# Attention and MLP in one kernel: w_out brought to one scale, both rows of a block bent at once, small factors on GpSimd, and a new order of the last products

## The chip, the cores and the metric

The kernel runs on one core of a Trainium2 chip. The core has TensorE (PE in the profile; its weight loads are PEld), VectorE (DVE), ScalarE (ACT), GpSimd (POOL) and SyncE (SP), which issues most DMAs. The metric is device microseconds of one execution, the median of several runs; lower is better.

## The reference

There are 8 batches of 12 heads, each with 448 rows of 64. Cut to what matters:

```python
scores = np.matmul(q, k.transpose(0, 1, 3, 2)) / np.sqrt(64) - np.log(448)
attn = np.matmul(1.0 / (1.0 + np.exp(-scores)), v)          # sigmoid, no softmax
x = attn.transpose(0, 2, 1, 3).reshape(3584, 768)
h = x @ w_in                                                # 768 x 2048
g = np.where(h >= 1, h, np.where(h <= -1, 0, (h + 1) ** 2 / 4))
out = g @ w_out                                             # 2048 x 768
```

## The kernel before, in words

**Numbers.** Products are made of f16 matmuls: each f32 factor is scaled by a power of two (found from its largest value) and split into a high and a low f16 part, and hi·hi, hi·lo and lo·hi are summed in PSUM. So each matrix product is three matmuls.

**Attention.** The 12 heads of a batch are 6 pairs, 48 in all. A pair has four pieces: three of 128 keys and one of 64. Scores of the first pairs are plain f32 matmuls (L407); later ones are L411, L416 and L425, of which L425 uses half the rows of the array (64). ScalarE makes the sigmoid (L454, L457), splits it (L465) and VectorE takes the low part (L466), which frees the PSUM bank of scores; there are two. The product with v is L498, which uses half the columns of the array (64). `prep_a` loads a pair (tile `raw`) and finds its largest values, on ScalarE (L344) for pairs below MAX_ACT and on VectorE (L346) for the others; `prep_b` makes the scales (L131 to L139, L359, L360) and splits q, k and v, on VectorE (L373, L374) or on GpSimd (L378 to L380). Corners of keys are copied on GpSimd (L437).

**The first product.** Of batches 0 and 1 it is plain (`up`, L722: chunk f of the 16 chunks of 128 columns of w_in against all six row chunks of x). From batch 2 (SB) on it is made of block products (`up_blocks`, L688): w_in chunks i and i + 8 and the two halves of x and of the 448 columns are combined so that 7 products of quarter size replace 8; each of the 8 values of i takes 63 matmuls of 224 columns, and the quarters are added up by VectorE (L697) and ScalarE. The combined weights are made once, during batch 1 (`mix`, L622 to L658), written to DRAM and loaded for each i (`load_set`, L664).

**Bending.** `bend` turns h into g, once for each chunk: ScalarE's Relu with scale ihr and bias hr (L735), VectorE's min and multiply (L736) and multiply and max (L737), ScalarE's f16 copy (L738), VectorE's low part (L739).

**The second product.** `down` (L758): six rows m of 128 outputs, for each eight units u; a unit is a pair of chunks of g (u and u + 8 from batch 2 on) with six matmuls. VectorE scales the result (L768), SP stores it.

**Scales.** The chunks of w_in and w_out form two groups (NA = 8), each with a scale of its own. The factors that this needs are 128x1 operations on VectorE, made by `small` (L553 to L557): for batch 1 in `common_scales`, from batch 2 on in `block_scales`, which calls it. `finish_x` and `finish_blocks` make the scale of x of the next batch first (L131 to L139, tiles x_e, x_s, x_i).

**Order.** The first stage loads and converts both weights (`convert`, L218 to L247; clamps at L226, on GpSimd or VectorE by CLAMP; `split`, L282 to L287), with the attention of batches 0 and 1 beside it. The main loop then goes over the batches: the units of the first product, then those of the second, and between them the pieces of the attention of the next batches, by a share. A scheduler orders each engine's instructions by priorities; blocks carry a raised one (Q_PRIO). Constants say how much of each kind goes to which engine and when.

Of the kernel before, what the change touches and what calls it, by code (L numbers as in the profile page):

```python
# [23 lines left out]
P = 128  # L24
# [12 lines left out]
NA = 8  # L37
# [13 lines left out]
MAX_ACT = 47  # L51
L0 = 9
# [4 lines left out]
CLAMP = 7  # L57
# [18 lines left out]
def sigmoid_attention_mlp(ctx: ExitStack, tc: tile.TileContext, first_qvk, qkv, w_in, w_out, out_t):  # L76
# [48 lines left out]
    def scales(m, n, tag, pool=None, square=False, less=0):  # L125

        pool = pool or sml_p
        few = {"bufs": 1} if tag == "x" else {}
        mask, top = (EXP_MASK - EXP_ONE, TOP - 1) if square else (EXP_MASK, TOP - less)
        e = sml_p.tile([P, 3], F32, tag="e", name=tag + "_e")[:, :n]  # L130
        nc.vector.tensor_scalar(out=e, in0=m, scalar1=TINY, scalar2=None, op0=ALU.max)  # L131
# [7 lines left out]
        nc.vector.tensor_scalar(  # L139
            out=inv.bitcast(I32), in0=ei, scalar1=float(top * EXP_ONE), scalar2=None, op0=ALU.subtract  # L140
        )
        return s, inv
# [9 lines left out]

    def all_sum(m, n, pm=None):

        mb = sml_p.tile([P, 3], BF16, tag="mb", name="mb", bufs=1)[:, :n]
        nc.vector.tensor_copy(out=mb, in_=m)
        if pm is None:
            pm = ps_mo.tile([P, 512], F32, tag="mo", name="pm")
        nc.tensor.matmul(pm[:, :n], ones, mb, start=True, stop=True)
        return pm[:, :n]  # L160
# [18 lines left out]
    class Weight:  # L179
# [74 lines left out]
        def find_scale(self):  # L254
# [298 lines left out]
    def small(tag, in0, s1, op0, s2=None, op1=None, ints=False):  # L553
        t = sml_p.tile([P, 1], F32, tag=tag, name=tag, bufs=2 if tag.startswith("od") else 1)
        o, i = (t.bitcast(I32), in0.bitcast(I32)) if ints else (t, in0)
        nc.vector.tensor_scalar(out=o, in0=i, scalar1=s1, scalar2=s2, op0=op0, **({"op1": op1} if op1 else {}))
        return t  # L557
# [108 lines left out]
    def block_scales(b, inv_x):  # L666

        common_scales(b, small("invq", inv_x, 0.25, ALU.mult), small("ihc", inv_x, mixed["inv"], ALU.mult))


    PRODUCTS = (0, 0, 0), (3, 4, 1), (5, 5, 2), (6, 3, 3), (1, 1, 0), (2, 6, 2), (4, 2, 3)

    def up_blocks(b, i, j):
# [20 lines left out]
        hf, hg = (rows[:, (i % 2 * 2 + k) * S : (i % 2 * 2 + k + 1) * S] for k in range(2))  # L694
# [3 lines left out]
        with tc.high_priority(offset=Q_PRIO):  # L698
# [3 lines left out]
            elif j == 3:  # L702
                add(u3, 2, u2)
                add(hg[:, HN:], 3, u3)
# [11 lines left out]
    def up(b, f, u):  # L716
# [23 lines left out]

    part = drm_p.tile([NCC, P, S], F32, name="part")

    def down(b, m, u, k):

        lo, hi = (0, NFC) if k is None else (GROUPS[k].start, GROUPS[k].stop)
        if u == 0:
            hold["po"] = ps_mo.tile([P, 512], F32, tag="mo", name="po")
            hold["o"] = out_p.tile([P, S], F32, tag="o", name="o")
            if m == 0:
                hold["od"] = down_sc[b, k]()  # L750
            if k == 1:
                nc.sync.dma_start(out=hold["o"], in_=part[m])
        po, o = hold["po"], hold["o"]
# [104 lines left out]
    for u, unit in enumerate(units):  # L858
# [108 lines left out]
```

## Time and profile before

| | us |
| --- | --- |
| median of 3 runs | 1190.68 |
| lowest and highest | 1190.14, 1194.91 |
| profiled execution | 1187.38 |
| its span | 1185.7 |
| PE busy | 1144.9 (97%) |
| DVE busy | 854.9 (72%) |
| ACT busy | 697.6 (59%) |
| POOL busy | 332.8 (28%) |

The span runs from the first to the last instruction of the profiled execution; its time has 1.7 us around that. The busy shares are averages over a first stage, in which weights are converted, and seven batches that repeat. The waits are those that the profile could find for each instruction, with what ended them. In the groups of instructions the number behind the bar is the busy time in all and the mean of one in ns. A timeline row gives start, length, engine, line, operation and, behind an x, how many in a row.

### The profile page before, as it was taken

The numbers are of one execution on the slowest core, as the hardware profiler recorded it, in microseconds if no ns is written. First come the engines' busy times: TensorE is split into PE (matmuls) and PEld (weight loads), VectorE is DVE, ScalarE is ACT, GpSimd is POOL, SyncE is SP. The second block draws the span as 40 slices with busy tenths as digits, with TensorE's granted clock in tenths as the row PEclk, the third lists the DMA queues.
The fourth block names the chain that finished last, engine by engine and source line by source line (L and its number), as shares of the span: only waits on it lengthen the run. The fifth ranks groups of instructions, "written<-read, shape, count | busy, mean of one in ns | idle before, by whom it ended". The sixth has DMA issues, their size and how long they took to land.

```text
span 1185.7 us, 20268 instructions
## 1 busy us (share of the span) xinstructions
PE 1144.9 (97%) x7662; PEld 669.3 (56%) x7662; DVE 854.9 (72%) x1828; ACT 697.6 (59%) x1158; POOL 332.8 (28%) x393
## 2 busy tenths in 40 slices
PE   5889899999999999999999999999999999999998
PEld 1224333444445776457754677557764577558954
DVE  6999999999956588457973689456884678736830
ACT  5886576665654577547864578455864476613510
POOL 3004410011323244234345235332532353310000
PEclk9899999999999999999999999999999999999999
DMA  9842354437542266224643065423552246302400
GB/s 367 322 153 76 118 161 152 134 119 257 182 148 72 95 217 210 76 72 142 238 163 102 30 236 208 135 64 128 204 211 64 65 147 220 126 24 87 163 16 32
DMA packets 58113, 170.01 MB, mean 143 GB/s; under 512 B 8608, under 2 KB 39840, under 8 KB 51872
## 3 DMA queue, kind: packets, MB, share of 16 engines
q1 hardware_dynamic: 56288, 159.29, 39.1%
q10 hardware_dynamic: 1728, 9.44, 2.2%
q8 instruction: 60, 0.98, 0.3%
q14 instruction: 37, 0.30, 0.1%
HBM read 126.94 MB, written 23.40 MB: 127 GB/s over the span
## 4 chain that ended last, share of the span: by engine, by line
PE 71%; DVE 17%; DMA 4%; ACT 3%; issue 2%; POOL 2%; SPq 0%; POOLq 0%; ACTq 0%; DVEq 0%
PE po L758 33%; PE ph L688 22%; PE pav L498 8%; PE psc L416 3%; PE psc L425 2%; PE ph L722 2%; DVE g L736 2%; PE psc L411 1%; DVE g L737 1%; DVE ghl L739 1%; DMA raw<-qkv 1%; DVE ahl L466 1%; DVE w_in_sb L244 1%; DVE mixa L632 1%; DVE w_out_sb L247 1%
## 5 line engine op out<-in xcount | busy, mean ns | idle before, releaser
L758 PE MATMUL po<-ghl,w_out_sb 128*128 128x448 f16 x2304 | 446.3, 353 | 1.5 <-DVE qkv_e L131 0.6
L758 PEld LDWEIGHTS <-w_out_sb 128*128 128x128 f16 x2304 | 221.7, 98 | 219.4 <-issue 15.9
L688 PE MATMUL ph<-w_in_sb 128*128 128x224 f16 x3024 | 307.7, 259 | 1.3 <-DVE g L737 0.9
L688 PEld LDWEIGHTS <-w_in_sb 128*128 128x128 f16 x3024 | 282.6, 98 | 30.1 <-issue 27.2
L466 DVE SCALAR_TENSOR_TENSOR ahl<-psc,ahl 128x896 f16<-128x896 f32 (+1 forms) x170 | 153.0, 900 | 105.7 <-ACT ahl L465 103.6
L378 POOL TENSOR_SCALAR raw<-raw,qkv_s 128x448 f32<-128x448 f32 (+1 forms) x93 | 71.0, 777 | 449.9 <-DVE qkv_i L139 346.3
L457 ACT ACTIVATE psc<-psc,nls,sqk 128x896 f32<-128x896 f32 (+1 forms) x136 | 129.5, 971 | 103.5 <-PE psc L425 86.6
L465 ACT ACTIVATE ahl<-psc 128x896 f16<-128x896 f32 (+1 forms) x170 | 126.9, 762 | 29.8 <-DVE ahl L466 28.6
L722 PE MATMUL ph<-xhl,w_in_sb 128*128 128x448 f16 x576 | 114.5, 356 | 4.7 <-DVE g L737 3.4
L344 ACT ACTIVATE dump<-raw 128x448 f16<-128x448 f32 (+1 forms) x105 | 61.9, 589 | 85.8 <-DMA raw<-qkv 84.5
L697 DVE TENSOR_TENSOR xhl<-ph,xhl 128x224 f32<-128x224 f32 x240 | 87.7, 383 | 25.3 <-PE ph L688 19.4
L738 ACT ACTIVATE ghl<-g 128x448 f16<-128x448 f32 x128 | 72.5, 573 | 44.2 <-DVE g L737 43.8
L498 PE MATMUL pav<-ahl,v 128*64 128x448 f16 x748 | 95.6, 360 | 0.0
L735 ACT ACTIVATE g<-xhl,hr,ihr 128x448 f32<-128x448 f32 x96 | 68.7, 752 | 41.9 <-DVE xhl L697 41.0
L722 PEld LDWEIGHTS <-w_in_sb 128*128 128x128 f16 x576 | 55.7, 99 | 63.6 <-issue 14.4
L736 DVE SCALAR_TENSOR_TENSOR g<-g,rk 128x448 f32<-128x448 f32 x112 | 81.4, 741 | 10.2 <-ACT g L735 10.0
L739 DVE TENSOR_TENSOR ghl<-g,ghl 128x448 f16<-128x448 f32 x128 | 85.0, 672 | 5.3 <-ACT ghl L738 4.8
L768 DVE TENSOR_SCALAR o<-po,od 128x448 f32<-128x448 f32 x48 | 32.5, 679 | 61.1 <-PE po L758 60.8
L380 POOL TENSOR_TENSOR hl<-raw,hl 128x448 f16<-128x448 f32 x62 | 71.1, 1167 | 0.0
L416 PE MATMUL psc<-qk 128*128 128x448 f16 x252 | 66.3, 354 | 2.0 <-ACT a L454 1.0
L737 DVE SCALAR_TENSOR_TENSOR g<-xhl,ihs,g 128x448 f32<-128x448 f32 x96 | 66.3, 708 | 0.3
L498 PEld LDWEIGHTS <-v 128*64 128x64 f16 x748 | 36.3, 109 | 37.9 <-issue 23.0
(167 smaller groups left out, 1198.5 us busy)
## 6 DMA issues: line engine op xcount, KB each, us to landing
w_in_sb<-blocks SPq DMA_DIRECT2D x48, 1344.0 KB, 6.1
raw<-qkv SPq DMA_DIRECT2D x34, 704.0 KB, 4.7
qk<-hl SPq DMA_DIRECT2D x320, 56.0 KB, 2.0
w_out_sb<-w_in SPq DMA_DIRECT2D x16, 768.0 KB, 8.5
out_t<-o SPq DMA_DIRECT2D x48, 224.0 KB, 1.9
blocks<-mixs SPq DMA_DIRECT2D x8, 768.0 KB, 3.5
w_out_sb<-w_out ACTq DMA_DIRECT2D x6, 768.0 KB, 4.1
raww<-w_out ACTq DMA_DIRECT2D x6, 768.0 KB, 5.7
```

The costliest lines, as they stand in the source:

```text
L416: nc.tensor.matmul(out, kq[:, j, 1, w], kq[:, j, 0, :], start=True, stop=False)
L457: nc.scalar.activation(a, a, AF.Sigmoid, bias=nls, scale=sqk)
L465: nc.scalar.activation(hi, x, AF.Copy, scale=ATT)
L466: nc.vector.scalar_tensor_tensor(out=lo, in0=x, scalar=ATT, in1=hi, op0=ALU.mult, op1=ALU.subtract)
L498: nc.tensor.matmul(pav[j * D : (j + 1) * D, :S], *terms[j][t], start=c == 0 and t == 0, stop=mid and t == len(terms[j]) - 1,)
L688: nc.tensor.matmul(out, w[:, wt, wh, c * P : (c + 1) * P], xc[:, xt, c, xh, :], start=j in (0, 2) and c + wh + xh == 0, stop=c == HC - 1 a ...
L697: add = lambda out, q, other: nc.vector.tensor_tensor(out=out, in0=quarter(q), in1=other, op=ALU.add)
L722: nc.tensor.matmul(ph[:, :S], w_in_sb[:, f, wh, c * P : (c + 1) * P], xhl[:, c, xh, :], start=c == 0 and wh + xh == 0, stop=c == NCC - 1 a ...
L736: nc.vector.scalar_tensor_tensor(out=g, in0=g, scalar=rt, in1=g, op0=ALU.min, op1=ALU.mult)
L737: nc.vector.scalar_tensor_tensor(out=g, in0=h, scalar=ihs, in1=g, op0=ALU.mult, op1=ALU.max)
L739: (nc.gpsimd if f % GPOOL else nc.vector).tensor_tensor(out=ghl[:, f, 1, :], in0=g, in1=hi, op=ALU.subtract)
L758: nc.tensor.matmul(po[:, :S], w_out_sb[:, f, wh, m * P : (m + 1) * P], ghl[:, f, gh, :], start=f == lo and wh + gh == 0, stop=f == hi - 1 ...
```

## The change

- **GpSimd's factors.** From batch 1 on `small` issues on GpSimd, but for the bitwise and.
- **One scale for w_out.** When w_out's scales are known, `even_out` makes a common one; during the blocks' first units of batch 2, `even_chunks` multiplies w_out's f16 parts in place to it, two chunks in one VectorE operation of 128x3072, eight in all. `block_scales` then needs one set of factors for both groups.
- **bend_two** bends rows i and i + 8 of a block in one go: each of its operations is 128x896, and the last additions of the block become one of 128x448. The quarters 2 and 3 change places.
- **Order of the second product.** From batch 2 on rows m = 0 and m = 1 take their units u = 0 to 5 first, then u = 6 and 7 of m = 0, then of m = 1.
- **Shares.** Three clamps of w_in (L226) and 48 corner copies (L437) go from GpSimd to VectorE, the largest values of eleven more pairs (MAX_ACT) from ScalarE to VectorE; L0, MIX1, WO_B and Q_PRIO shift loads, mixing, conversion and priorities.

```diff
-WO_B = 66
+WO_B = 63
-MAX_ACT = 47
-L0 = 9
+MAX_ACT = 36
+L0 = 17
-CLAMP = 7
+CLAMP = 1
-CORN = 10
+CORN = 38
+TE = 4
+CUT = 6
+TWO = 0
+EV0 = 12
-MIX1 = 85
-Q_PRIO = 72
+MIX1 = 95
+Q_PRIO = 12
...
-        nc.vector.tensor_scalar(out=o, in0=i, scalar1=s1, scalar2=s2, op0=op0, **({"op1": op1} if op1 else {}))
+        (nc.gpsimd if state.get("late") and TE & 4 and op0 != ALU.bitwise_and else nc.vector).tensor_scalar(out=o, in0=i, scalar1=s1, scalar2=s2, op0=op0, **({"op1": op1} if op1 else {}))
...
-        common_scales(b, small("invq", inv_x, 0.25, ALU.mult), small("ihc", inv_x, mixed["inv"], ALU.mult))
+        invq, ihc = small("invq", inv_x, 0.25, ALU.mult), small("ihc", inv_x, mixed["inv"], ALU.mult)
+        rt = small("qm", *(largest(invq, k)[1] for k in range(2)), ALU.min)
+        up_sc[b, 0] = up_sc[b, 1] = sc = up_scales(ihc, rt, 0)
+        od = small("od", inverse("ig", sc[4]), even["inv"], ALU.mult)
+        down_sc[b, None] = lambda: od
...
+    def even_chunks(f, n):
+        w = w_out_sb[:, f : f + n].rearrange("p f h n -> p (f h n)")
+        k = int(f >= NA)
+        nc.vector.tensor_scalar(out=w, in0=w, scalar1=evens[:, 2 + k : 3 + k], scalar2=None, op0=ALU.mult)
...
-    PRODUCTS = (0, 0, 0), (3, 4, 1), (5, 5, 2), (6, 3, 3), (1, 1, 0), (2, 6, 2), (4, 2, 3)
+    PRODUCTS = (0, 0, 0), (3, 4, 1), (5, 5, 3), (6, 3, 2), (1, 1, 0), (2, 6, 3), (4, 2, 2)
...
-                add(hg[:, :HN], 2, u2)
-                add(hf[:, HN:], 3, u2)
+                both = h[:, HN : HN + S].rearrange("p (r n) -> p r n", r=2)
+                halves = hold[i, 2].rearrange("p (r n) -> p r n", r=2)[:, :, :HN]
+                other = u2.rearrange("p (r n) -> p r n", r=1).to_broadcast([P, 2, HN])
+                nc.vector.tensor_tensor(out=both, in0=halves, in1=other, op=ALU.add)
         if j == 6:
-            bend(b, i + NFC // 2, hg)
-            bend(b, i, hf)
+            bend_two(b, i, h)
+
+    def bend_two(b, i, h):
+
+        ihr, hr, rt, ihs, _ = up_sc[b, 0]
+        g = raw_p.tile([P, 2 * DM], I32, tag="raww", name="g2").bitcast(F32)[:, : 2 * S]
+        hi, lo = (ghl[:, i :: NFC // 2, k, :] for k in range(2))
+        g2 = g.rearrange("p (r n) -> p r n", r=2)
+        nc.scalar.activation(g, h, AF.Relu, bias=hr, scale=ihr)
+        nc.vector.scalar_tensor_tensor(out=g, in0=g, scalar=rt, in1=g, op0=ALU.min, op1=ALU.mult)
+        nc.vector.scalar_tensor_tensor(out=g, in0=h, scalar=ihs, in1=g, op0=ALU.mult, op1=ALU.max)
+        nc.scalar.activation(hi, g2, AF.Copy)
+        nc.vector.tensor_tensor(out=lo, in0=g2, in1=hi, op=ALU.subtract)
...
-        return [lambda m=m, u=u: down(b, m, u, k) for m in range(NCC) for u in range(n // 2)]
+        order = [(m, u) for m in range(NCC) for u in range(n // 2)]
+        if b >= SB:
+
+            first = [(m, u) for m in range(2) for u in range(CUT)] + [(m, u) for m in range(2) for u in range(CUT, n // 2)]
+            order[: n] = first
+        return [lambda m=m, u=u: down(b, m, u, k) for m, u in order]
...
+                if b == SB and u >= EV0 and (u - EV0) % 4 == 0 and (u - EV0) // 4 < NFC // 2:
+                    even_chunks((u - EV0) // 4 * 2, 2)
```

The change also moves instructions that it does not name, since the scheduler orders anew. In the pieces below the lines are those of the kernel that each piece is of: L425, L416, L498 and L688 of before are L433, L424, L506 and L719 after it.

On TensorE, in the blocks of batch 6, a piece of attention in before (psc is a bank of scores, ph a block's bank; tiles hl and qk are split keys and queries):

```order
11890 L416 MATMUL psc<-qk 128x448
11891 L416 LDWEIGHTS qk
11892 L416 MATMUL psc<-qk 128x448
11893 L425 LDWEIGHTS hl
11894 L425 MATMUL psc<-hl 128x448
11895 L688 LDWEIGHTS w_in_sb
11896 L688 MATMUL ph<-w_in_sb 128x224
```

The same place after the change (pav is the bank of the product with v):

```order
11890 L424 MATMUL psc<-qk 128x448
11891 L424 LDWEIGHTS qk
11892 L424 MATMUL psc<-qk 128x448
11893 L433 LDWEIGHTS hl
11894 L433 MATMUL psc<-hl 128x448
11895 L433 LDWEIGHTS hl
11896 L433 MATMUL psc<-hl 128x448
11897 L506 LDWEIGHTS v
11898 L506 MATMUL pav<-ahl,v 64x448
```

In before one half-row matmul stands alone between blocks, and its fellow follows 18 block matmuls later; after, the two stand together and the products with v follow them.

On VectorE, at the end of batch 1's second product, in before:

```order
613 L556 TENSOR_SCALAR od<-qq 128x1
614 L768 TENSOR_SCALAR o<-po,od 128x448
615 L556 TENSOR_SCALAR ihs_3411<-ihc,sg_3409 128x1
616 L768 TENSOR_SCALAR o<-po,od 128x448
617 L156 CAST mb<-m_3674 128x3
618 L466 SCALAR_TENSOR_TENSOR ahl<-psc,ahl 128x896
```

And after the change (L699 is the new scaling, L831 was L768, L164 was L156, L474 was L466):

```order
582 L831 TENSOR_SCALAR o<-po,od 128x448
583 L699 TENSOR_SCALAR w_out_sb<-w_out_sb,evens 128x3072 x7
584 L831 TENSOR_SCALAR o<-po,od 128x448
585 L699 TENSOR_SCALAR w_out_sb<-w_out_sb,evens 128x3072
586 L164 CAST mb<-m_3663 128x3
587 L474 SCALAR_TENSOR_TENSOR ahl<-psc,ahl 128x896
```

The factors for the next batch are gone from this place, and the eight scalings stand around batch 1's last result.

On GpSimd, at the start of batch 1, two rows stood in before for the last chunk of w_out:

```order
15 L282 TENSOR_SCALAR w_out_sb<-w_out_sb,wo_s 128x768
16 L284 TENSOR_TENSOR w_out_sb<-w_out_sb 128x768
17 L437 COPY w_in_sb<-hl 64x2x64 x6
18 L378 TENSOR_SCALAR raw<-raw,qkv_s 128x448 x2
19 L378 TENSOR_SCALAR raw<-raw,qkv_s 128x512
```

After the change the factors (L564, was L556) stand between them; the end of them:

```order
32 L564 TENSOR_SCALAR hr_1798<-rk_1790 128x1
33 L564 TENSOR_SCALAR sg_1802<-rk_1800 128x1
34 L564 TENSOR_SCALAR ihr_1806<-ih_1776,rk_1800 128x1
35 L564 TENSOR_SCALAR hr_1808<-rk_1800 128x1
36 L564 TENSOR_SCALAR od<-gb 128x1
37 L564 TENSOR_SCALAR ihs_1794<-ih_1768,sg_1792 128x1
38 L564 TENSOR_SCALAR ihs_1804<-ih_1776,sg_1802 128x1
39 L292 TENSOR_TENSOR w_out_sb<-w_out_sb 128x768
40 L386 TENSOR_SCALAR raw<-raw,qkv_s 128x448 x2
```

22 factors stand between the two operations on w_out (L290 and L292, which were L282 and L284), 15 of them up to and with the first hr; the corner copies (L437) are gone from GpSimd here.

More of the change, by code (lines that the diff above doesn't have):

```diff
@@ L130, in scales @@
         e = sml_p.tile([P, 3], F32, tag="e", name=tag + "_e")[:, :n]
+        eng = nc.gpsimd if tag == "qkv" and TE & 1 else nc.vector
         nc.vector.tensor_scalar(out=e, in0=m, scalar1=TINY, scalar2=None, op0=ALU.max)
@@ L666, in block_scales, with even_out @@
     def block_scales(b, inv_x):
-        common_scales(b, small("invq", inv_x, 0.25, ALU.mult), small("ihc", inv_x, mixed["inv"], ALU.mult))
-    PRODUCTS = (0, 0, 0), (3, 4, 1), (5, 5, 2), (6, 3, 3), (1, 1, 0), (2, 6, 2), (4, 2, 3)
+        invq, ihc = small("invq", inv_x, 0.25, ALU.mult), small("ihc", inv_x, mixed["inv"], ALU.mult)
[3 more added lines that the diff above has]
+        down_sc[b, None] = lambda: od
+    even = {}
+    evens = const.tile([P, 4], F32, name="evens")
+    def even_out():
+        low = evens[:, 0:1]
+        nc.vector.tensor_scalar(out=low, in0=wo.scale[0], scalar1=wo.scale[1], scalar2=None, op0=ALU.min)
+        even["inv"] = evens[:, 1:2]
+        nc.vector.tensor_scalar(out=even["inv"], in0=wo.inv[0], scalar1=wo.inv[1], scalar2=None, op0=ALU.max)
+        for k in range(2):
+            nc.vector.tensor_scalar(
+                out=evens[:, 2 + k : 3 + k], in0=low, scalar1=wo.inv[k], scalar2=None, op0=ALU.mult
+            )
+    def even_chunks(f, n):
[3 more added lines that the diff above has]
+    PRODUCTS = (0, 0, 0), (3, 4, 1), (5, 5, 3), (6, 3, 2), (1, 1, 0), (2, 6, 3), (4, 2, 2)
     def up_blocks(b, i, j):
@@ L692, in up_blocks @@
                 )
-        hf, hg = (rows[:, (i % 2 * 2 + k) * S : (i % 2 * 2 + k + 1) * S] for k in range(2))
+        h = rows[:, i % 2 * 2 * S : (i % 2 * 2 + 2) * S]
+        hf, hg = h[:, :S], h[:, S:]
         u2, u3 = (rows[:, 4 * S + i % 2 * S + k * HN : 4 * S + i % 2 * S + (k + 1) * HN] for k in range(2))
@@ L702, in up_blocks @@
             elif j == 3:
[L703 to L704 removed]
+                add(u3, 3, u2)
+                add(hg[:, HN:], 2, u3)
             elif j == 4:
@@ L725, in up @@
                 )
-        if u == NCC // 2 - 1:
+        if u == NCC // 2 - 1 and not TWO:
             bend(b, f, ph[:, :S])
+        elif u == NCC // 2 - 1:
+            bend_next(b, f, ph[:, :S])
     def bend(b, f, h):
@@ L739, in bend, with bend_next @@
         (nc.gpsimd if f % GPOOL else nc.vector).tensor_tensor(out=ghl[:, f, 1, :], in0=g, in1=hi, op=ALU.subtract)
+    def bend_next(b, f, h):
+        ihr, hr, rt, ihs, _ = up_sc[b, int(f >= NA)]
+        if f % 2 == 0:
+            hold["g"] = raw_p.tile([P, 2 * DM], I32, tag="raww", name="g2").bitcast(F32)[:, : 2 * S]
+        g, r = hold["g"], f % 2
+        gf = g[:, r * S : (r + 1) * S]
+        nc.scalar.activation(gf, h, AF.Relu, bias=hr, scale=ihr)
+        nc.vector.scalar_tensor_tensor(out=gf, in0=gf, scalar=rt, in1=gf, op0=ALU.min, op1=ALU.mult)
+        nc.vector.scalar_tensor_tensor(out=gf, in0=h, scalar=ihs, in1=gf, op0=ALU.mult, op1=ALU.max)
+        if r == 1:
+            hi, lo = (ghl[:, f - 1 : f + 1, k, :] for k in range(2))
+            g2 = g.rearrange("p (r n) -> p r n", r=2)
+            nc.scalar.activation(hi, g2, AF.Copy)
+            nc.vector.tensor_tensor(out=lo, in0=g2, in1=hi, op=ALU.subtract)
     part = drm_p.tile([NCC, P, S], F32, name="part")
@@ L751, in down @@
             if k == 1:
-                nc.sync.dma_start(out=hold["o"], in_=part[m])
-        po, o = hold["po"], hold["o"]
+                nc.sync.dma_start(out=hold["o", m], in_=part[m])
+        po, o = hold["po", m], hold["o", m]
         pair = (u, u + NFC // 2) if b >= SB else (lo + 2 * u, lo + 2 * u + 1)
@@ L891, in sigmoid_attention_mlp @@
     inv_x = finish_x(1)
+    state["late"] = True
     common_scales(1, inv_x)
```

24 lines of the change are left out of this document (13 added, 11 removed).

## The prediction

> **What bounds the kernel now.** I read the page first, for the share of each engine and the chain that ended last.
>
> ```profile
> span 1185.7 us, 20268 instructions
> PE 1144.9 (97%) x7662; PEld 669.3 (56%) x7662; DVE 854.9 (72%) x1828; ACT 697.6 (59%) x1158; POOL 332.8 (28%) x393
> PE 71%; DVE 17%; DMA 4%; ACT 3%; issue 2%; POOL 2%; SPq 0%; POOLq 0%; ACTq 0%; DVEq 0%
> ```
>
> TensorE (PE) is busy 97% of the span, so what is not TensorE's own work can be worth some 40 us at most. The chain gives VectorE (DVE) 17%, so I asked next for the engines' busy time by stretches of the span.
>
> ```profile
> 12.00:40.00 28.00, 20.81 (x68) 4.83 (x65) 27.16 (x40) 18.63 (x30) 6.83 (x3) 0.82 1.03 407
> 40.00:92.00 52.00, 43.05 (x178) 11.60 (x178) 50.52 (x105) 45.08 (x66) 0.00 (x0) 0.93 0.59 203
> 205.00:248.00 43.00, 38.39 (x193) 17.97 (x192) 40.56 (x100) 24.11 (x33) 4.26 (x2) 0.96 0.40 141
> 248.00:320.00 72.00, 72.00 (x402) 35.17 (x400) 67.52 (x130) 48.79 (x82) 11.89 (x14) 1.00 0.59 197
> ```
>
> The columns are the stretch, its length, the busy time of PE, PEld, DVE, ACT and POOL, the clock, the DMA share. Up to about 248 us DVE is full (27.16 of 28, 40.56 of 43 us); from 248 us on PE is (72.00 of 72). So there are two regimes: before 248 us a microsecond of DVE counts, after it a microsecond of PE. The table of PE's waits says what is left of PE's idle time.
>
> ```profile
> PE ph L722 <- DVE g L737: 3.4, 3, 1.8
> PE pm L159 <- DVE g L737: 3.2, 2, 2.6
> PE ph L688 <- DVE g L737: 0.9, 1, 0.9
> PE ph L688 <- DVE xhl L697: 0.4, 1, 0.4
> ```
>
> The rows on L722 and L159 lie in the first regime. In the block products, L688, where most of the edits are, PE waits 0.9 and 0.4 us in all. So bend_two, one scale for w_out and GpSimd's small factors give nothing there by being cheaper; they can only spoil something. The last place at which DVE stops PE is here:
>
> ```profile
> 231.71 3.00 PE L722 MATMUL ph<-xhl,w_in_sb 128*128 128x448 f16 x15
> 238.64 0.16 PE L159 MATMUL pm<-mb,one 128*128 128x3 bf16 x1 [0.63 <-DVE g L737]
> 240.63 8.65 PE L722 MATMUL ph<-xhl,w_in_sb 128*128 128x448 f16 x36 [1.82 <-DVE g L737]
> ```
>
> After this idle time 36 matmuls take 8.65 us, 0.240 each, where 15 took 3.00, 0.200 each: the pause costs another 1.4 us in a slower clock.
>
> **The change part by part. First the order on PE.** From 248 us on the time is the number of PE's slots, so I looked for what a slot costs in different orders.
>
> ```profile
> 504.00 0.92 PE L416 MATMUL psc<-qk 128*128 128x448 f16 x4
> 504.85 0.55 PE L425 MATMUL psc<-hl 64*128 64x448 f16 x4
> 505.33 1.14 PE L498 MATMUL pav<-ahl,v 128*64 128x448 f16 x10
> 506.40 0.93 PE L758 MATMUL po<-ghl,w_out_sb 128*128 128x448 f16 x4
> 545.63 0.94 PE L498 MATMUL pav<-ahl,v 128*64 128x448 f16 x7
> 546.51 1.23 PE L688 MATMUL ph<-w_in_sb 128*128 128x224 f16 x11
> 984.74 0.36 PE L425 MATMUL psc<-hl 64*128 64x448 f16 x1
> 985.03 1.90 PE L688 MATMUL ph<-w_in_sb 128*128 128x224 f16 x18
> ```
>
> From start to start, four full matmuls (L416) take 0.85 us, four with half the rows (L425) 0.48, ten with half the columns (L498) 1.07, seven of these 0.88 and a single L425 0.29. That fits 0.189 us a slot, two half matmuls to a slot, and about 0.096 us for each change between full, half rows and half columns: 4 × 0.189 + 0.096 = 0.85; 2 × 0.189 + 0.10; 5 × 0.189 + 0.12; four slots for seven; one whole slot for a single one, 0.189 + 0.10. So an odd half matmul wastes half a slot, 0.0945 us, and each change of shape 0.096.
>
> I counted both in the instruction orders of before and after, by batch of block products (the order in which the scheduler slips attention between them is new). Changes of shape and odd leftovers: batch 2, 63 to 60 and 12 to 6; batch 3 the same; batch 4, 63 to 56 and 12 to 4; batch 5, 63 to 57 and 12 to 0; batch 6, 54 to 51 and 10 to 0; batch 7 no attention, no difference. Batch 2: 3 × 0.096 + 6 × 0.0945 = 0.85; the five are 0.85, 0.85, 1.43, 1.71 and 1.23, together −6.07 us. Between 240 and 394 us the same count gives +0.58 (0.48 − 0.19 + 0.29). Net **−5.5 us**. Nothing covers or uncovers this: PE does not wait there.
>
> **The start, up to 240 us.**
>
> ```profile
> L226 DVE TENSOR_SCALAR w_in_sb<-w_in_sb 128x768 f32<-128x768 f32 x4 | 2.2, 559 | 0.5 <-ACT w_in_sb L224 0.4
> L556 DVE TENSOR_SCALAR sg<-rk 128x1 f32<-128x1 f32 x14 | 2.9, 204 | 0.0
> L437 POOL COPY w_in_sb<-hl 64x128 f16<-64x128 f16 x68 | 32.3, 474 | 45.5 <-DVE hl L374 43.6
> L959 POOL MEMSET const-float32-0.0<- 128x1 f32 x1 | 0.1, 99 | 0.3 <-issue 0.3
> 220.85 0.14 DVE L139 TENSOR_SCALAR x_i<-x_e 128x1 int32<-128x1 int32 x1
> 233.13 0.15 DVE L556 TENSOR_SCALAR hr<-rk 128x1 f32<-128x1 f32 x1
> ```
>
> Three clamps go from POOL to DVE, 3 × 0.559 = 1.7 us; a DVE wait of 0.5 on the POOL clamps goes; with reordered work of 0.5 that puts the scale of x for batch 1 at +1.7. Then 21 small factors leave DVE. One lasts 204 ns but the next starts about 125 ns later, so −2.6, and the first L737 of batch 1 comes 0.9 earlier; PE restarts with it, about **−1.0 us** (bounds −2.5, if nothing but the factors moves, and +1.5, if the clamps alone count).
>
> On POOL the price of a 128x1 factor is in no row. The nearest from below is a 128x1 fill, 0.10 us, from above the 64x128 copy, 0.474; I take 0.3, between them. 15 of them lie ahead of hr: 4.5 us against the 12.3 us (220.85 to 233.13) that DVE takes for them between other work, so hr is not later unless one costs over 0.8 us. In the later batches the same chain, ten POOL factors to hr, has 26 us from x_i to the first L735, as here for batch 3:
>
> ```profile
> 517.66 0.14 DVE L139 TENSOR_SCALAR x_i<-x_e 128x1 int32<-128x1 int32 x1
> 543.68 1.41 ACT L735 ACTIVATE g<-xhl,hr,ihr 128x448 f32<-128x448 f32 x2 [0.65 <-DVE xhl L697]
> ```
>
> There it costs nothing up to 2 us each. The 48 corner copies that leave POOL reach DVE after this place, where DVE has room, and cost nothing. L0 = 17 pushes two early loads back behind others in the stretch where the DMA share is 1.03; they are used first after 90 us, so nothing.
>
> **One scale of w_out.** Eight new DVE operations of 3072 f16 elements, queued on DVE behind the end of batch 1's downs and ahead of L466, which frees PE's score banks. Their price is in no row.
>
> ```profile
> L655 DVE TENSOR_SCALAR mixp<-w_in_sb,mixes 128x768 f16<-128x768 f16 x16 | 7.3, 494 | 0.1
> L655 DVE TENSOR_SCALAR mixp<-w_in_sb,mixes 128x384 f16<-128x384 f16 x16 | 4.3, 314 | 0.0
> L466 DVE SCALAR_TENSOR_TENSOR ahl<-psc,ahl 128x896 f16<-128x896 f32 x102 | 110.7, 1085 | 97.8 <-ACT ahl L465 97.6
> L737 DVE SCALAR_TENSOR_TENSOR g<-ph,ihs,g 128x448 f32<-128x448 f32 x32 | 21.6, 676 | 0.1
> 391.94 0.68 DVE L768 TENSOR_SCALAR o<-po,od 128x448 f32<-128x448 f32 x1 [8.27 <-PE po L758]
> 395.74 1.74 DVE L466 SCALAR_TENSOR_TENSOR ahl<-psc,ahl 128x896 f16<-128x896 f32 x2 [2.27 <-ACT ahl L465]
> 400.49 0.54 PE L416 MATMUL psc<-qk 128*128 128x448 f16 x2
> ```
>
> From below, L655's slope: (494 − 314) / 384 = 0.47 ns an element, 0.494 + 2304 × 0.47 ns = 1.57 us, eight 12.6. From above, the slope of L737 and L466: (1085 − 676) / 448 = 0.91 ns, 0.676 + 2624 × 0.00091 = 3.07 us, eight 24.6. I take 1.57, since L655 is the same operation on the same types. They start at 383.8, where DVE begins its 8.27 us of idle time; seven end at 394.8, then L768 (0.68) and the eighth, until 397.0; L466 starts some 1.5 us late. PE writes the score banks again at 400.49, 3.0 us after L466's end at 397.48, so the cover holds: 0. The Trainium skill, "VectorE: DVE Perf Modes", section "Side-by-side: where the cycles go for N=2048 bf16", says that such a one-source 16-bit operation in SBUF can run at four elements a cycle; an estimate by that page for 3072 is 0.97 us, which would hide them still better and leave the sum as it is; the 494 ns row shows half that rate, so I keep the row.
>
> **bend_two and the maxima.** One 896-wide operation at 1.085 us replaces two at 0.68 to 0.74 (rows of L466 and L737), on DVE about 0.3 us less for each of three, nothing on PE. The end of the block, where both rows' results come together, is a little later; in the last batch, u = 6 and 7 are put off behind 12 units of six matmuls, 12 × 6 × 0.189 = 13.6 us, of which some 8 come after the last block's products, which covers the chain of five wide operations (5.7 to 7.7 us): 0. Eleven more pairs have their maxima (L346) on DVE, where the one such pair of before waited for its load:
>
> ```profile
> 985.47 1.68 DVE L346 TENSOR_REDUCE m<-raw 128x2 f32<-128x896 f32 x2 [2.74 <-DMA raw<-qkv]
> 990.42 1.89 PE L688 MATMUL ph<-w_in_sb 128*128 128x224 f16 x18 [0.36 <-DVE xhl L697]
> L344 ACT ACTIVATE dump<-raw 128x448 f16<-128x448 f32 (+1 forms) x105 | 61.9, 589 | 85.8 <-DMA raw<-qkv 84.5
> ```
>
> All of DVE's queue stood behind it for 2.74 us, and PE lost 0.36 at L688 five microseconds later. ACT waited 84.5 us in such loads without harm. For each of the eleven the bounds are 0 and 1.2 us (this wait and those of the next 15 us, seen here); most fall where DVE has a third of its time free, so I take **+0.5 us** for all.
>
> **Sum.** −1.0 − 5.5 + 0.5 = −6.0 us on the profiled execution: 1187.4 becomes 1181.4. That execution lies 3.3 under the median of the runs, so I take the difference to the median: 1190.7 − 6.0 = **1184.7 us**, which is −0.50%, just at what a measurement of this kernel can tell from no change (0.5%, 6 us).
>
> **The rivals.** *The room on DVE pays too.* If the restart gains 2.5 us and the waits of L688 and half of the 3.4 at L722 go: −5.5 − 2.5 − 1.3 = −9.3, 1181. For it speaks that DVE loses some 15 us of work; against it that PE hardly waits. *The maxima on DVE cost.* Half of eleven at 1.2 us is +6.6: −6.5 + 6.6, 1191, no change; all of them, +13.2, gives 1197. Against it: the wait of 2.74 cost PE 0.36 at once. *GpSimd's factors are slow.* If each of the 15 ahead of hr has to wait out a wide DVE operation of about 0.95 us and then takes 0.3, hr comes 18.8 us after x_i (+1.7): 241.4, 8.3 later than before; less 1.0 no longer gained, PE loses 8.3 and about 1.4 in clock: −5.0 + 9.7, 1195, within 0.5%. The Trainium skill states such a rule ("SBUF — State Buffer", section "Who interferes with whom": a DVE operation with two SBUF inputs holds up a GpSimd one that reads SBUF to its end). The trace bears on it only loosely: no row here shows such small operations on GpSimd.
>
> *Slower: scaling w_out in place is dear.* At 3.07 us, eight last from 383.8 to 409.0 with L768 in between; L466 is 13.3 late, less 3.0 of cover, PE stands about 10.5 us and another 1.4 to 1.7 in clock: −6.0 + 12.2, 1196.9 us. It decides from (395.74 + 3.0 − 383.8 − 0.7) / 8 = 1.8 us an operation. For it: no row has an f16 operation of this length; against it: L655's rate. That the change does not do what it says is not a rival: the order shows the new sequence.
>
> **How the numbers follow.** The forecast has 0.50, its own spread 2.5 us to both sides, so 0.27 faster and 0.23 same. Room on DVE 0.15, faster. Maxima 0.15 same and 0.04 slower. GpSimd's factors 0.07, same. Scaling dear 0.09, slower. That makes faster 0.42, same 0.45, slower 0.13. The range leaves out the two slower cases (0.13), the GpSimd case's upper end and the end of the best one: 1180 to 1194.
>
> **What would show it.** In the changed profile the first L688 of one batch must follow that of the batch before about 1 us sooner, with no single L425 between blocks from batch 5 on; the eight scalings should last 1.6 us each, end before 398 and be followed by no PE wait; GpSimd's factors should be under 0.5 us and the first L735 of batch 1 not after 234; L346 should wait without PE waiting behind it. I am wrong if the batches from 394 us on are no shorter, or if a PE wait over 3 us appears at 240, 397 or in a downs half.

## The result, and the profile after

The changed kernel takes 1209.8 us (median of 4 runs, 1206.0 to 1212.2), the kernel before in the same series 1191.2: a ratio of 1.0147, 95% interval 1.0113 to 1.0182. It is slower by 18.6 us, where 1184.7 and a range up to 1194 had been forecast. The profiled execution of it has these totals:

```profile
span 1204.3 us, 19842 instructions
PE 1146.1 (95%) x7662; PEld 669.9 (56%) x7662; DVE 870.3 (72%) x1560; ACT 660.5 (55%) x996; POOL 368.5 (31%) x455
```

PE has as much work as before (1146.1 against 1144.9) in a span that is 18.6 us longer. So it stands more. The first matmuls of the batches tell where. Between the first block matmul of batch 2 and the end of PE's work lie 787.2 us before and 802.8 after, 15.7 of the 18.6; the other 2.9 were lost ahead of batch 2. I took each of these times apart in the way of the prediction: slots (0.189 and 0.096 us a matmul, 0.096 a change of shape, a half slot for an odd half matmul), PE's waits over 0.1 us, and what is left.

| us, batches 2 to 7 | time | slots | waits | rest |
| --- | --- | --- | --- | --- |
| before | 787.2 | 779.6 | 2.2 | 5.4 |
| after | 802.8 | 773.5 | 17.9 | 11.4 |

The slots fell by 6.1 us, as forecast. The waits rose by 15.7 and the rest by 6.0. The largest of PE's waits from 394 us on, after (before they were four, of 0.9 us at most):

```profile
PE psc L424 <- DVE qkv_e L137: 6.0, 3, 2.1
PE ph L719 <- DVE xhl L743: 4.2, 6, 1.1
PE ph L719 <- DVE xhl L729: 3.2, 5, 1.3
PE psc L419 <- DVE ahl L474: 2.2, 4, 0.7
PE psc L424 <- DMA qk<-hl: 1.4, 2, 0.8
```

They lie in batches 2, 3 and 4 (4.4, 4.7 and 4.7 us); 5 and 6 have 1.3 and 2.2. The largest, in batch 2's second product, in PE's timeline after:

```profile
486.38 0.54 PE L424 MATMUL psc<-qk 128*128 128x448 f16 x2 [0.22 <-issue]
486.85 0.36 PE L433 MATMUL psc<-hl 64*128 64x448 f16 x2
489.28 0.55 PE L424 MATMUL psc<-qk 128*128 128x448 f16 x2 [2.06 <-DVE qkv_e L137]
489.76 0.36 PE L433 MATMUL psc<-hl 64*128 64x448 f16 x2
490.06 2.02 PE L506 MATMUL pav<-ahl,v 128*64 128x448 f16 x10
492.01 8.30 PE L821 MATMUL po<-ghl,w_out_sb 128*128 128x448 f16 x39
```

And the same piece of attention before:

```profile
481.85 0.92 PE L416 MATMUL psc<-qk 128*128 128x448 f16 x4
482.70 0.55 PE L425 MATMUL psc<-hl 64*128 64x448 f16 x4
483.18 1.14 PE L498 MATMUL pav<-ahl,v 128*64 128x448 f16 x10
484.25 8.12 PE L758 MATMUL po<-ghl,w_out_sb 128*128 128x448 f16 x42
```

Before, two score tiles are filled at one go; after, the second one waits 2.06 us for its bank. Then the ten products with v take 2.02 us instead of 1.14: the clock. In the stretches 486 to 490 and 490 to 493.4 us after (the column behind POOL's is the granted clock):

```profile
486.00:490.00 4.00, 1.71 (x9) 0.50 (x8) 3.25 (x10) 1.92 (x3) 0.20 (x1) 1.00 0.00 0
490.00:493.40 3.40, 3.40 (x16) 1.27 (x15) 0.01 (x1) 3.21 (x4) 3.40 (x7) 0.52 0.01 2
```

With half the clock for some 3.4 us, this wait of 2.06 us costs nearly 4. That is a part of the rest in the table: the granted clock is 0.50 in two stretches of 3.41 us in batches 2 to 7, this one and one at 633.5 us, which is 1.7 us each and 3.4 of the 6.0. What the other 2.6 are is not shown. What the bank waits for is a chain through four engines, here in order of time:

```profile
474.01 1.16 POOL L388 TENSOR_TENSOR v<-raw,v 128x512 f16<-128x512 f32 x1
...
480.66 0.58 ACT L352 ACTIVATE dump<-raw 128x448 f16<-128x448 f32 x1 [3.35 <-DMA raw<-qkv]
...
481.93 1.67 ACT L465 ACTIVATE psc<-psc,nls,sqk 128x896 f32<-128x896 f32 x2
...
484.27 0.17 DVE L164 CAST mb<-m 128x3 bf16<-128x3 f32 x1 [4.59 <-ACT dump L352]
...
486.08 1.08 DVE L757 TENSOR_TENSOR ghl<-g,ghl 128x896 f16<-128x896 f32 x1
...
489.06 0.16 DVE L137 TENSOR_SCALAR qkv_e<-psc 128x3 f32<-128x3 f32 x1
```

GpSimd ends a split at 475.2, and the next load into that tile is issued at 475.9; ScalarE stands 3.35 us at the maxima of that load, with the sigmoid L465 behind; VectorE stands 4.59 us at the cast behind the maxima; and L137, which frees the bank, comes behind all that. One of bend_two's wide operations, L757, stands in the chain too, between two of VectorE's operations on scores.

The other steps: the eight scalings of w_out, and GpSimd's last factor that the restart needs, with the restart itself:

```profile
386.94 7.83 DVE L699 TENSOR_SCALAR w_out_sb<-w_out_sb,evens 128x3072 f16<-128x3072 f16 x7 [0.45 <-PE po L821]
...
395.48 1.01 DVE L699 TENSOR_SCALAR w_out_sb<-w_out_sb,evens 128x3072 f16<-128x3072 f16 x1
...
231.60 0.98 POOL L564 TENSOR_SCALAR hr<-rk 128x1 f32<-128x1 f32 x1
...
240.35 4.89 PE L767 MATMUL ph<-xhl,w_in_sb 128*128 128x448 f16 x25 [1.06 <-DVE g L784]
```

### The profile page after: what moved, and what is told of

Read it like the earlier page. It is cut to its first block, busy times and chain, and to the rows that moved or that the text cites. A ratio compares the mean times of both kernels' runs of the same rounds, so it can differ in the third digit from the quotient of the medians.

```text
span 1204.3 us, 19842 instructions
## 1 busy us (share of the span) xinstructions
PE 1146.1 (95%) x7662; PEld 669.9 (56%) x7662; DVE 870.3 (72%) x1560; ACT 660.5 (55%) x996; POOL 368.5 (31%) x455
## 5 line engine op out<-in xcount | busy, mean ns | idle before, releaser
L719 PE MATMUL ph<-w_in_sb 128*128 128x224 f16 x3024 | 306.5, 259 | 7.8 <-DVE xhl L743 4.2
L719 PEld LDWEIGHTS <-w_in_sb 128*128 128x128 f16 x3024 | 283.8, 98 | 37.1 <-issue 34.6
L386 POOL TENSOR_SCALAR raw<-raw,qkv_s 128x448 f32<-128x448 f32 (+1 forms) x93 | 75.0, 821 | 453.2 <-issue 133.1
L474 DVE SCALAR_TENSOR_TENSOR ahl<-psc,ahl 128x896 f16<-128x896 f32 (+1 forms) x170 | 152.7, 900 | 62.2 <-ACT ahl L473 59.7
L465 ACT ACTIVATE psc<-psc,nls,sqk 128x896 f32<-128x896 f32 (+1 forms) x136 | 129.2, 971 | 113.5 <-PE psc L433 107.5
L506 PE MATMUL pav<-ahl,v 128*64 128x448 f16 x748 | 94.6, 365 | 0.0
L753 ACT ACTIVATE g<-xhl,hr,ihr 128x896 f32<-128x896 f32 x48 | 54.4, 1133 | 69.4 <-DVE xhl L743 68.4
L831 DVE TENSOR_SCALAR o<-po,od 128x448 f32<-128x448 f32 x48 | 32.6, 680 | 69.8 <-PE po L821 69.3
L424 PE MATMUL psc<-qk 128*128 128x448 f16 x252 | 67.0, 356 | 10.5 <-DVE qkv_e L137 6.0
L754 DVE SCALAR_TENSOR_TENSOR g<-g,qm 128x896 f32<-128x896 f32 x48 | 62.5, 1302 | 12.6 <-ACT g L753 12.6
L352 ACT ACTIVATE dump<-raw 128x448 f16<-128x448 f32 (+1 forms) x72 | 42.4, 589 | 51.6 <-DMA raw<-qkv 50.7
L756 ACT ACTIVATE ghl<-g 128x896 f16<-128x896 f32 x48 | 45.5, 948 | 45.1 <-DVE g L755 45.0
L445 DVE COPY w_in_sb<-hl 64x128 f16<-64x128 f16 x48 | 30.1, 627 | 53.1 <-POOL hl L388 52.8
L757 DVE TENSOR_TENSOR ghl<-g,ghl 128x896 f16<-128x896 f32 x48 | 55.8, 1162 | 10.7 <-ACT ghl L756 10.1
L729 DVE TENSOR_TENSOR xhl<-ph,xhl 128x224 f32<-128x224 f32 x144 | 54.7, 384 | 8.0 <-PE ph L719 4.5
L415 PE MATMUL psc<-ghl 64*128 64x448 f32 (+1 forms) x128 | 37.2, 669 | 21.8 <-ACT a L462 17.6
```

Source lines behind the costliest of these rows:

```text
L386: nc.gpsimd.tensor_scalar(out=rt, in0=rt, scalar1=s[:, t : t + 1], scalar2=1.0, op0=ALU.mult, op1=ALU.mult)
L424: nc.tensor.matmul(out, kq[:, j, 1, w], kq[:, j, 0, :], start=True, stop=False)
L465: nc.scalar.activation(a, a, AF.Sigmoid, bias=nls, scale=sqk)
L474: nc.vector.scalar_tensor_tensor(out=lo, in0=x, scalar=ATT, in1=hi, op0=ALU.mult, op1=ALU.subtract)
L506: nc.tensor.matmul(pav[j * D : (j + 1) * D, :S], *terms[j][t], start=c == 0 and t == 0, stop=mid and t == len(terms[j]) - 1,)
L719: nc.tensor.matmul(out, w[:, wt, wh, c * P : (c + 1) * P], xc[:, xt, c, xh, :], start=j in (0, 2) and c + wh + xh == 0, stop=c == HC - 1 a ...
```

## The experiments

Each row of this table is a kernel of its own, with its median, its ratio to the kernel before on the same chip, and the parts of batches 2 to 7 in its profiled execution.

| | median | ratio, interval | slots | waits | rest |
| --- | --- | --- | --- | --- | --- |
| corners back | 1210.7 | 1.0151 (1.0124 to 1.0177) | 771.8 | 19.7 | 12.6 |
| idle copies | 1208.7 | 1.0140 (1.0117 to 1.0164) | 771.8 | 18.7 | 12.4 |
| bends apart | 1201.3 | 1.0071 (1.0043 to 1.0099) | 777.6 | 10.0 | 6.9 |
| maxima back | 1218.9 | 1.0222 (1.0199 to 1.0245) | 774.4 | 21.2 | 15.7 |
| all maxima on VectorE | 1206.6 | 1.0136 (1.0111 to 1.0161) | 774.4 | 13.9 | 9.1 |
| bends apart, corners back | 1192.6 | 1.0013 (0.9993 to 1.0033) | 777.0 | 5.4 | 5.8 |
| scale and bend_two alone | 1214.7 | 1.0210 (1.0163 to 1.0256) | 772.9 | 24.2 | 13.4 |
| scale alone | 1194.3 | 1.0031 (1.0019 to 1.0043) | 776.8 | 4.8 | 5.0 |
| ScalarE narrow | 1213.2 | 1.0196 (1.0176 to 1.0217) | 773.9 | 22.0 | 11.1 |
| VectorE narrow | 1216.4 | 1.0216 (1.0194 to 1.0239) | | | |
| all narrow, shared tile | 1201.0 | 1.0090 (1.0063 to 1.0116) | 776.0 | 14.3 | 7.9 |
| scale, bend_two, CUT | 1219.4 | 1.0237 (1.0201 to 1.0272) | 772.1 | 25.8 | 14.9 |
| fixed order, bend_two | 1223.7 | 1.0283 (1.0234 to 1.0332) | 763.9 | 34.9 | 19.6 |
| fixed order, bends apart | 1225.0 | 1.0290 (1.0257 to 1.0324) | 763.9 | 42.1 | 16.6 |
| fixed order, before | 1203.6 | 1.0110 (1.0082 to 1.0139) | 763.9 | 27.2 | 9.1 |
| fixed order, apart, maxima back | 1206.8 | 1.0128 (1.0106 to 1.0150) | 763.9 | 30.7 | 9.2 |
| apart, corners and maxima back | 1188.7 | 0.9984 (0.9970 to 0.9998) | 776.8 | 5.4 | 5.1 |
| apart, corners back, VectorE's factors | 1192.7 | 1.0000 (0.9983 to 1.0017) | 777.0 | 6.7 | 5.6 |

The trace of the run with VectorE narrow is of an execution of 3046 us, in which the matmuls took about twice as long as in the others, so its parts are left out.

**First theory: the corner copies.** After the change VectorE stands 52.8 us in 17 waits at corner copies (L445), for GpSimd's split, and nearly all of them lie in batches 1 to 4, where most of the loss is.

```diff
-CORN = 38
+CORN = 10
```

> The changed kernel, with CORN = 10 again: the 48 corner copies are on GpSimd as before, all else is as changed. Theory 1 (VectorE stands in its queue behind GpSimd's split when a corner copy is next, 52.8 us in 17 waits, and the scores' banks come free late): the waits of PE in batches 2 to 4 go (about 5.5, 6 and 4 us) and the one of 2.4 us with its slow clock at 322 us, so 1209.8 becomes 1190 to 1196. Theory 2 (the 896-wide operations of bend_two make each block end late): 1206 to 1210, since the copies themselves last only 0.2 us. Theory 3 (the maxima on VectorE wait for their loads): 1206 to 1210.

Measured 1210.7. The wait of 2.4 us at 322 us went (from there to batch 2 this run loses nothing against the kernel before, the changed kernel 3.7), but batches 2 to 4 stayed as long, with other waits, the largest of them:

```profile
PE pav L506 <- DVE ahl L474: 5.1, 3, 2.1
PE psc L424 <- DVE qkv_e L137: 3.8, 2, 1.9
PE ph L719 <- DVE xhl L729: 3.5, 4, 1.3
```

The theory falls as the cause of the whole. Its form with idle copies adds, to the above:

```diff
+                    if p < 38:
+                        nc.vector.tensor_copy(out=ident[rows, :], in_=ident[rows, :])
```

> As the run with the corner copies back on GpSimd, and at each of the 48 places VectorE also makes a copy of the same shape (64x128, two bytes) of a constant tile onto itself, which waits for no other engine. Theory 1 in its form that the wait is the cost: as that run, within 2 us. If it is VectorE's time for the copies, or their place in its queue, that costs: 1200 or more.

Measured 1208.7, as with the copies and without them. The stop near 322 us was there again (a wait of 3.0 us, 4.1 lost up to batch 2). But it does not hang on VectorE's copies: the kernel below with the bends apart and the corner copies on GpSimd has none of them, and PE stands 3.2 us at the same matmul. What brings this stop and takes it away stays open.

**Bends apart, and maxima back.**

```diff
-            bend_two(b, i, h)
+            bend(b, i + NFC // 2, hg)
+            bend(b, i, hf)
```

> The changed kernel, but rows i and i + 8 of a block are bent apart again, in five 448-wide operations each (the last addition stays one of 448). Theory 1: 1206 to 1212, the corner copies still stand there. Theory 2: 1192 to 1197, the waits of L719 for L743 and of ScalarE for L743 and L755 go.

Measured 1201.3: without bend_two about half of the loss is gone, neither the first theory's number nor the second's.

```diff
-MAX_ACT = 36
+MAX_ACT = 47
```

> The changed kernel, with MAX_ACT = 47 again: the maxima of eleven pairs (36 to 46) are on ScalarE as before. Theory 1: 1204 to 1210; batches 5 and 6 come 1 to 2 us each closer to the count of slots, batches 2 to 4 stay. Theory 3: 1192 to 1197.

Measured 1218.9, 9 us longer: with bend_two, the maxima on VectorE are worth something. The third theory falls here.

```diff
-MAX_ACT = 36
+MAX_ACT = 22
```

> The changed kernel with MAX_ACT = 22: the maxima of pairs 22 to 35 go to VectorE too, so ScalarE makes none during the block products. Theory 4 (in the second products of batches 2 to 4 ScalarE waits in its queue for a load, its maxima hold back the sigmoid, and the scores' bank comes free late: 4.1, 4.6 and 2.1 us; pairs 36 and up, whose maxima are on VectorE, show no such place): these go, 1197 to 1202. Theory 2 (the wide operations of bend_two are late whatever the maxima do): 1206 to 1212.

Measured 1206.6. Taking ScalarE's maxima out of the chain shown above shortens batches 3 and 4 by 3.4 and 1.3 us, but not batch 2; other waits take their place. Theory 4 explains a part at most.

**The two edits together, and bend_two alone.** CORN = 10 and the bends apart:

> The changed kernel with the two rows of a block bent apart and the corner copies on GpSimd. Against the 1201.3 of the bends apart alone: 1197 to 1199 if VectorE's corner copies cost the wait at 322 us with its slow clock (3.6 us, gone with the corners back, there again with the idle copies); 1200 to 1202 if the gain at that place is lost again later, as it was with the corners back alone.

Measured 1192.6, below both expectations and not to be told from the kernel before: without these two edits the whole loss is gone. The gain is not at 322 us, where this kernel stops as well (3.2 us), but in batches 2 to 7, which are 6.4 us shorter than with the bends apart alone. The corner copies cost 8.7 us by the medians (6.9 by the ratios) where the bends are apart, and nothing where they are not. The reverse, with WO_B, MAX_ACT, L0, CLAMP, CORN, MIX1 and Q_PRIO as before, TE = 0 and CUT = 8:

> Of the change only the one scale of w_out, the block scales that need it and bend_two with its quarters; the shares, loads, maxima, corners, clamps, priorities, the order of the second products and VectorE's small factors are those of before. Theory 2: 1200 to 1204, all of the 8 to 11 us that bending apart took away. Theory 4: 1198 or more too, since the maxima are on ScalarE. If bend_two hurts only together with the moved shares: 1188 to 1193.

> As the run before, with the two rows bent apart: of the change only the one scale of w_out is left, the eight scalings among it. All theories: 1188 to 1194, as before.

Measured 1214.7 and 1194.3: bend_two costs 20 us with the old shares too. One scale by itself costs 0.3%. In the first of the two the second product waits for the last bent rows:

```profile
PE po L821 <- ACT ghl L756: 11.0, 4, 3.0
```

The new order of the second product is there to cover that (CUT = 6 in that kernel):

> The kernel with only the one scale and bend_two of the change (1214.7), and the new order of the second product's first two rows (CUT = 6). Its trace has PE wait 11.0 us in 4 places for the last block's bent rows at the second product, each with a slow clock behind it; the order should cover them: 1214.7 less 11 to 17, 1197 to 1204. If these waits only move to another place: 1210 or more.

Measured 1219.4. That wait does go from the list, but the sum of waits does not fall (24.2 to 25.8): other waits have come in its place.

**Is it the width?** With CORN = 10, bend_two's operations are cut into 448-wide ones on ScalarE, on VectorE, or on both, such as

```diff
-        nc.scalar.activation(g, h, AF.Relu, bias=hr, scale=ihr)
+        for r in (1, 0):
+            p = slice(r * S, (r + 1) * S)
+            nc.scalar.activation(g[:, p], h[:, p], AF.Relu, bias=hr, scale=ihr)
```

> The changed kernel with the corner copies back on GpSimd (1210.7), and in bend_two ScalarE's two operations cut into 448-wide ones, row by row, while VectorE's three stay 896 wide. Theory 5 (an 896-wide operation of VectorE stands too long ahead of what frees the scores' bank and slows GpSimd's split, which has two SBUF inputs beside it): 1206 to 1212. Theory 6 (ScalarE's wide operations stand ahead of the sigmoid): 1192 to 1198.

> As the run with ScalarE's operations cut, the other way round: VectorE's three operations are cut into six 448-wide ones, ScalarE's two stay 896 wide. Theory 5: 1192 to 1199. Theory 6: 1206 to 1212.

> All five operations of bend_two cut into 448-wide ones, row after row, but in the one shared tile of bend_two with its two buffers; corner copies on GpSimd. If the width does it: 1191 to 1195, as with the bends apart and the corners back (1192.6). If the shared tile (both rows' buffer comes free only together, two buffers where the bends apart had three) does it: 1204 or more.

Measured 1213.2, 1216.4 and 1201.0. Cutting the operations of one engine alone does not help (theories 5 and 6 both fall), and all narrow but in one tile lies in the middle. Each of these kernels has another order on TensorE, since the scheduler orders by its own forecast of all engines. Only in batches 5 and 6 does the last one have the order (by kinds of matmul) of the kernel with the bends apart and the corners back, and there it takes the same time (138.6 and 132.8 us against 138.6 and 132.9); in batches 2 to 4 and 7, where the order is another, it is 2 to 3 us longer in each. So the shared tile showed no price where the order was the same.

**Is it the order on TensorE?** From batch 2 on TensorE takes the order of the program text:

```diff
-PM = 9
+PM = 2
```

> The changed kernel with the corner copies back on GpSimd, and TensorE's order from batch 2 on that of the program text instead of the scheduler's (PM = 2): each piece's scores and products with v stand together, 42 changes of shape a batch and no odd half matmul. Theory 7 (the scheduler's order on TensorE, which bend_two's durations moved, makes the waits): as the next run, within 3 us. Theory 8 (the wide operations make the waits on whatever order): 8 to 18 us over the next run.

> The same fixed order on TensorE, matmul for matmul, with the two rows of a block bent apart. By slots alone this order is 3 us a batch shorter than that of before (63 to 42 changes, 12 to 0 odd ones), 1178 to 1182, if the waits stay at those of the bends apart (0.8 us a batch); if closer-standing scores wait for their two banks, 1190 or more.

> The kernel before with the same fixed order on TensorE from batch 2 on. If the order alone makes or saves waits: as the run before it, within 5 us. If the shares of the change (maxima, loads, GpSimd's factors) matter in it: apart by more.

Measured 1223.7, 1225.0 and 1203.6. With one and the same order of matmuls, bend_two and the bends apart do not differ in the whole, where the scheduler's orders put 18 us between them (1210.7 and 1192.6, corners back in both). Batches 2 and 3 are 1.8 and 2.4 us longer with the wide operations, with the same sum of waits (5.1 us a batch) and, other than with the bends apart, stretches at half clock; later ones are shorter. This speaks for the order that the scheduler made with bend_two as the source of the 18 us, as theory 7 has it, but does not show it. The fixed order has 35 to 42 us of waits of its own, in which a price could hide, and it fixes TensorE alone and not the other engines. Nor does one order give one sum of waits: in batch 5 the changed kernel and three others with bend_two (corners back, idle copies, all maxima on VectorE) have the same order by kinds of matmul, and waits of 1.3, 2.9, 3.9 and 0.6 us.

Fewest slots are not the shortest time either: the kernel before with the fixed order has 16 us less in slots than without it and 25 more in waits. That the changed shares take 21 us longer than the shares of before under this order was new. Between 810 and 950 us, in batch 5, the waits of the kernel with the fixed order and the bends apart are

```profile
PE ph L719 <- DVE xhl L729: 8.0, 3, 5.4
PE psc L424 <- DVE qkv_e L137: 5.0, 2, 3.5
```

With MAX_ACT = 47 in it, the order on TensorE being the same matmul for matmul:

> The fixed order with the bends apart (1225.0) and the maxima of pairs 36 to 46 back on ScalarE; TensorE's order is the same, matmul for matmul. If VectorE standing at a maximum for its load holds back what the blocks need (L719 waits up to 5.4 us in batches 4 to 6, none such in the kernel before under this order): 1202 to 1207. If not: 1222 or more.

Measured 1206.8, and in the same stretch

```profile
PE ph L719 <- DVE xhl L729: 2.1, 2, 1.5
PE psc L419 <- DVE mb L164: 1.6, 1, 1.6
```

So under this order VectorE's maxima cost 18 us: with them, VectorE stands for loads (21.9 us in 10 waits) with the blocks' additions behind. Standing alone is not the price: in the scheduler's order, with the bends apart and the corners back, VectorE stands 20.0 us in 8 such waits, and PE waits 5.4 us in all from batch 2 on.

**The terms that were left**, in the scheduler's order, bends apart and corners back: MAX_ACT = 47, and TE = 0.

> The changed kernel with the bends apart, the corner copies on GpSimd (1192.6) and the maxima of eleven pairs on ScalarE again, in the scheduler's order. If the maxima on VectorE cost whatever the order: 1184 to 1189. If it depends on the order (with bend_two, putting them back made it 9 us longer): 1191 or more.

> The changed kernel with the bends apart, the corner copies on GpSimd (1192.6), and the small factors on VectorE again (TE = 0). By the prediction's own term (2.6 us of VectorE ahead of the restart at 240 us): 1194 to 1196. If they are hidden: 1191 to 1193.

Measured 1188.7 and 1192.7. Without bend_two the maxima on VectorE cost 3.9 us (0.3%); the factors on GpSimd are worth nothing that can be told from zero. The first of these two is the best kernel of all: 0.9984 of the kernel before (0.9970 to 0.9998), just clear of it; as the lowest of 18 it may owe that to chance.

## Why the prediction was wrong, point by point

- **The order on PE, −5.5 us: the step that failed.** The count was right: 6.1 us fewer slots in the block batches against 6.07 forecast, and in the kernel before time, slots and waits agree within 1.2 us a batch. Wrong was the sentence behind it, "Nothing covers or uncovers this: PE does not wait there." PE did not wait in the kernel before, and I carried that over to a kernel with another order and other durations. The runs show 15.7 us of new waits in its place, and 6.0 of rest, of which 3.4 are slow clock behind two such waits. The next two terms, both put at nothing, are the edits that brought the loss: without them the kernel takes 1192.6 us. What is left of the change is then worth nothing that can be told from zero (0.9993 to 1.0033), and not the −6.0 us of the sum.
- **bend_two at nothing on PE.** It cost 8.5 us in the changed kernel, 18 with the corners back and 20 with the old shares. Under one fixed order it cost nothing in the whole, which points to the order that the scheduler made for it, without showing it. The argument that cheaper work off the bottleneck gives nothing held; its second half, that such edits can spoil something, was written down and then priced at 0.
- **The corner copies at nothing.** I priced their duration and not that VectorE stands at them for GpSimd's split. With the bends apart they cost 7 to 9 us: VectorE stands there 45.5 us in 11 waits, and PE waits 7.4 us from batch 2 on for VectorE's L474, which frees the scores' banks, against 1.2 with the copies on GpSimd. The order is another one too, so the two are not separated. With bend_two the copies' cost is lost among the other waits.
- **The maxima, +0.5 us, and the rival that they cost.** Their sign depends on the order: −9 us with bend_two, +3.9 with the bends apart, +18 in the fixed order. The mechanism of the rival, VectorE standing for a load with the blocks behind, is the one seen in the fixed order. Nor do ScalarE's waits for loads stay without harm: in the chain at 480 us one of them holds up the scores.
- **The scaling of w_out.** 1.01 us for the eighth and 7.83 for seven, 1.0 to 1.1 each instead of 1.57. They end at 396.5, no PE wait follows, and the slower rival did not come. The Trainium skill, "VectorE: DVE Perf Modes", section "Side-by-side: where the cycles go for N=2048 bf16", gave 0.97 us as an estimate: with 1.01 the trace agrees to within some 5%, and the slope from the shorter row was too dear.
- **The start, −1.0 us.** PE restarted at 240.35 instead of 240.63, and the matmul that stood at 245.71 came at 243.75: 0.3 us from the restart and 1.7 from the slow clock, which came at 241.2 us before and not after. GpSimd's hr came at 231.6, not later than before, so the rival on its factors did not come either. But its factors took 0.2 to 1.3 us each, not under 0.5, and the first Relu of batch 1 (L735 before, L782 after) came at 235.4, where the prediction had set 234 as the limit. Putting the factors back changed nothing in the whole (1192.7 against 1192.6), so the forecast gain is not shown by any run's time.
- **Up to 394 us, +2.9.** A wait of 2.4 us at 322 us with the slow clock behind it. It was not forecast, and since it comes and goes with corner copies on either engine, its cause is open. The first block matmul of batch 2 stands at 393 to 403 us in these traces, so 2.9 us is not much here.

What in the scheduler's order makes the waits stays open. In batches 2 to 4, in the scheduler's orders, fewer changes of shape go with more waits (54 to 62 a batch with 2.5 to 5.5 us, 63 or 64 with 1.1 at most), but batch 5 of the changed kernel has 57 and waits of 1.3. A kernel with bend_two under the order of the bends apart was not tried.

## What to carry to other kernels

A count of work on the bottleneck holds only as long as its waits stay what they were. When a scheduler makes the order, a change of a duration on any engine can make a new one, with other waits: compare the two also under one fixed order, and remember that the waits of that order can hide a price. Take single edits out of a change that lost, and take them out in pairs too: here two edits held the loss, and one of them showed a cost only without the other. Where engine queues are this full, an operation that must wait for a load or for another engine (a maximum, perhaps a corner copy) is to be priced by what stands behind it as well as by its length.

## What the runs showed of the hardware that had not been expected

The granted clock goes to half in steps. After the change its stretches at 0.50 that start between 140 and 640 us last 3.41 us each, and their starts (145.41, 322.91, 490.16 and 633.52 us) lie whole multiples of 3.413 us apart. In batches 2 and 3 such a stretch followed where PE had worked 1.35 us of the 3.41 before it on this grid, with no wait longer than 2.1 us; 1.85 us did not bring one (the column behind POOL's is the granted clock):

```profile
486.75:490.16 3.41, 1.35 (x9) 0.41 (x10) 2.50 (x9) 1.61 (x2) 0.36 (x1) 1.00 0.00 0
490.16:493.57 3.41, 3.41 (x15) 1.26 (x15) 0.00 (x0) 3.36 (x4) 3.41 (x7) 0.50 0.04 10
773.47:776.88 3.41, 1.85 (x16) 0.71 (x16) 2.16 (x8) 1.10 (x2) 1.39 (x3) 1.00 0.00 0
776.88:780.29 3.41, 3.41 (x21) 1.68 (x18) 0.00 (x0) 3.35 (x5) 3.41 (x6) 1.00 0.14 34
```

By these rows what a wait costs may depend on where it falls on the grid. After much the same waits at 147 us (one of 2.58 us in each), the same 24 matmuls took three times in the profiled executions. Before:

```profile
146.68 4.70 PE L722 MATMUL ph<-xhl,w_in_sb 128*128 128x448 f16 x24 [0.90 <-DVE g L737]
```

After:

```profile
147.01 5.58 PE L767 MATMUL ph<-xhl,w_in_sb 128*128 128x448 f16 x24 [0.49 <-DVE g L784]
```

And with the corner copies back, whose first 150 us are the same program:

```profile
148.67 7.51 PE L767 MATMUL ph<-xhl,w_in_sb 128*128 128x448 f16 x24 [0.83 <-DVE g L784]
```

On each trace's grid PE had worked 1.89, 1.36 and 1.85 us of the 3.41 before, and none, one and two stretches at half clock followed. So the busy time alone does not decide it; what else does is not shown. A spread of 2.8 us at one place is within that between the runs of one kernel (1190.1 to 1194.9 us before), so differences under 3 us in the first stage say little.
